# New order tables for the four engines of a decode kernel with two attention and two MLP layers

## The chip, the cores and the metric

The kernel runs on one core of a Trainium2 chip. Its time is the device time in microseconds (us), as the median of several executions. A core has five engines that run side by side, each through its own list of instructions in order: PE (TensorE, matrix products), DVE (VectorE), ACT (ScalarE), POOL (GpSimd) and SP (SyncE, which here issues the loads). They wait for each other with semaphores. Sixteen DMA engines move data between the chip's memory (DRAM) and the core's own memory (SBUF); PE writes its results into eight banks of PSUM.

## What is computed

Eight sequences with one new token each (x is 8 x 448) go through attention, MLP, and the same attention and the same MLP again, each with a layer norm ahead of it and its input added:

```
def _A_ref(x, k_cache, v_cache, wq, wo):       # Hq 16, Hkv 8, Dh 256
    W = min(4096, max(256, Sk // 4))           # the last 1024 of 4096 keys
    q = (x @ wq).reshape(B, Sq, Hq, Dh)
    scores = einsum("bhqd,bhkd->bhqk", q, k) * (Dh ** -0.5)
    p = softmax(scores)
    return einsum("bhqk,bhkd->bhqd", p, v).reshape(B, Sq, Hq * Dh) @ wo
def _B_ref(x, w1, w2):
    return silu(x @ w1) @ w2
x = x + _A_ref(layernorm(x), K, V, wq, wo);  x = x + _B_ref(layernorm(x), w1, w2)
x = x + _A_ref(layernorm(x), K, V, wq, wo);  x = x + _B_ref(layernorm(x), w1, w2)
```

Both attention layers read the same K and V. These are 8 sequences x 8 heads x 1024 keys x 256 numbers in bfloat16, for K and for V: 128 pieces of 512 KB. With the weights, 77.7 MB are read.

## The kernel before

**Tiling.** A batch b is one of the eight sequences. Its 16 pieces (8 of K, then 8 of V, one a key head) are loaded once, each into one of 33 slots of SBUF; both layers use them while they are there. Piece number n goes to slot n mod 33, so a load waits until the piece 33 places earlier, from two batches before, has been read for the last time. `pump` hands out the slots; SP issues the loads in the order of the sequence: x, wq, K of batch 0, wo, V of batch 0, w1, w2, then K and V of batches 1 to 7.

**Stages of a batch**, with the names that the text uses (`name@b` is the task of batch b):

- `KHk` (L591): each K piece is transposed in its slot by DVE, in two halves, as 32x32 blocks; 16 half transposes a batch.
- `S0.0`, `S0.1` (L611): scores of the first layer for heads 0 to 3 and 4 to 7, four tasks of 8 matmuls each. They use the query `qbd`, which for the first layer POOL spreads out (`qbd1`, L580).
- softmax: `max0`, `mT0`, `mg0`, `mb0` on DVE (L625 to L629), `exp0` on ACT (L632), `perm0` on PE (L634), `turn0` on DVE (L638), `l0` on PE (L640) and `rl0`, the reciprocals, on DVE (L643).
- values: `PV0` (two tasks, L667) and `PV4` to `PV7` (L678) on PE; `oev0`, `oevt` on ACT (L648), `oT0`, `oTt` on PE (L649), `oTev0`, `oTevt` on DVE (L652) bring the result into columns. In the last batch `PVc` and `oTc7` (L689, L694) take the last head.
- `wo` (four tasks, L736), `rowb1` (ACT, L1074), `fold1` (PE, L475), and in the last batch `woc` (L752).
- the MLP, `chain`: `xb1` (DVE, L766), `stat1`, `w1` (PE, L774, L486), `var1`, `tanh` (ACT), `pow1` (POOL, L781), `yT`, `hT` (DVE, L501, L790), `w2` (two tasks, PE, L807), `rowb2` (ACT, L811), `fold2` (PE), `xb2` (DVE), `x2b` (ACT).
- the second layer's query: `stat2`, `wq0`, `wq1` (PE, L832), `rmask` (ACT, L819), `qTa`, `qm0`, `qm1` (DVE, L501, L840), `qd` (PE, L843), `qbdw` (ACT, L847).
- the second layer: `S1.0`, `S1.1` (L611), its softmax (`max1` to `rl1`) and its values (`PV1.0`, `PV1.1`, two tasks each, L702), `oev1`, `oT1`, `oTev1`.

The second layer's wo and MLP are done for batches 0 to 5 together (`wo8`, `rowb8`, `xinit8`, `fold8`, `x8b`, `xc8`, `sq8`, `sqh8`, `stat8`, `w18`, `yT8`, `z8`, `h8`, `w28`, `rowb9`, `fold9`) and for 6 and 7 as a pair (`woL` and the names with an L, `xr`, `xres`). The last batch's second layer works on two groups of heads with their own softmax (`maxg1`, `maxg0` and so on). `idle` tasks are matmuls of 512 columns whose result nobody reads.

**Order.** The program adds its tasks in the order in which they are written. For each of PE, DVE, ACT and POOL a table, `ORDER` (L16), then says in which order that engine runs its own: each character is the place (0 to 9, a to z, A to Z) of the next task in the list of those still left. `Plan.schedule` reads the tables, and `Plan.emit` works out the semaphore waits that the dependencies need. The two score buffers, the PSUM banks and the slots are shared, so two tasks that use the same one depend on each other in program order; the tables can only move tasks between such constraints. A bank counts as in use by one engine at a time, so a read by ACT also waits for a read of the same bank by DVE. An engine never passes over a task that isn't ready.

## Time and profile before

| | us |
|---|---|
| median of 3 runs (lowest, highest) | 232.49 (232.43, 232.64) |
| the profiled execution | 232.87 |
| its span, first to last instruction | 231.1 |

| engine | busy us | share of the span |
|---|---|---|
| PE | 161.0 | 70% |
| DVE | 142.2 | 62% |
| ACT | 55.1 | 24% |
| POOL | 22.7 | 10% |

The busy sums say which engine works most, not what holds the kernel up. To see that, one looks at stretches of the span and at the waits. The profile's views used here: the page, with rows of 40 equal slices (5.8 us each) and the groups of instructions; the table of stretches (busy time, granted PE clock, share of the DMA engines and GB/s between two moments); the timeline, in which neighbouring instructions of one kind are merged, and the last bracket of a row is the engine's idle time before it and what ended it; the waits; and the chain of work that ended last. `L` and a number is a line of the kernel, and many tasks share the line of a helper.

### The profile page before, as it was taken

The numbers are of one execution on the slowest core, as the hardware profiler recorded it, in microseconds if no ns is written. First come the engines' busy times: TensorE is split into PE (matmuls) and PEld (weight loads), VectorE is DVE, ScalarE is ACT, GpSimd is POOL, SyncE is SP. The second block draws the span as 40 slices with busy tenths as digits, with TensorE's granted clock in tenths as the row PEclk, the third lists the DMA queues.
The fourth block names the chain that finished last, engine by engine and source line by source line (L and its number), as shares of the span: only waits on it lengthen the run. The fifth ranks groups of instructions, "written<-read, shape, count | busy, mean of one in ns | idle before, by whom it ended". The sixth has DMA issues, their size and how long they took to land.

```text
span 231.1 us, 7935 instructions
## 1 busy us (share of the span) xinstructions
PE 161.0 (70%) x3539; PEld 86.0 (37%) x3539; DVE 142.2 (62%) x398; ACT 55.1 (24%) x140; POOL 22.7 (10%) x41
## 2 busy tenths in 40 slices
PE   0261071854897868886887779769878877899883
PEld 0060030321363336333543353335435333565542
DVE  6828935012984696559639945983995796343623
ACT  2200000122012322132223212332322223325341
POOL 1110111000002003000300110120003000000201
PEclk9999999995559999889999999999999999999998
DMA  6999999999999999999899999999999999400000
GB/s 237 379 357 407 382 393 406 405 341 410 405 408 413 415 408 407 410 406 408 355 362 415 408 367 406 413 410 354 415 414 405 396 409 410 189 3 3 3 3 4
DMA packets 22829, 78.22 MB, mean 338 GB/s; under 512 B 2430, under 2 KB 5388, under 8 KB 22412
## 3 DMA queue, kind: packets, MB, share of 16 engines
q1 hardware_dynamic: 22772, 77.71, 86.2%
q8 instruction: 28, 0.46, 0.8%
q10 hardware_dynamic: 24, 0.01, 0.1%
q14 instruction: 5, 0.04, 0.0%
HBM read 77.70 MB, written 0.01 MB: 336 GB/s over the span
## 4 chain that ended last, share of the span: by engine, by line
PE 36%; DVE 29%; SPq 16%; DMA 9%; ACT 5%; issue 3%; POOL 0%; DVEq 0%; ACTq 0%
DVE slot L591 20%; SPq L443 10%; PE bank L611 10%; DMA w_sb<-in_B_w_dram 6%; SPq L403 5%; PE bank L702 4%; PE bank L667 3%; PE bank L832 3%; PE bank L736 2%; DVE bank L501 2%; PE bank L678 2%; DMA slot<-in_A_k_cache_dram 2%; ACT qbd L847 2%; PE bank L486 2%; DVE mm L625 1%
## 5 line engine op out<-in xcount | busy, mean ns | idle before, releaser
L591 DVE STREAM_TRANSPOSE slot<-slot 128x512 uint32<-128x512 uint32 x128 | 80.7, 679 | 7.9 <-DMA slot<-in_A_k_cache_dram 7.5
L611 PE MATMUL bank<-slot,qbd 128*8 128x256 bf16 (+1 forms) x1024 | 42.0, 300 | 14.1 <-DVE slot L591 10.4
L611 PEld LDWEIGHTS bank<-slot,qbd 128*8 128x8 bf16 (+1 forms) x1024 | 26.9, 98 | 24.7 <-DVE slot L591 13.8
L781 POOL TENSOR_TENSOR fcols<-fcols 128x1 f32<-128x1 f32 x16 | 8.7, 546 | 147.6 <-ACT fcols L779 147.6
L632 ACT ACTIVATE E<-bank,mm 128x256 bf16<-128x256 f32 x17 | 8.1, 474 | 46.9 <-DVE mm L629 41.1
L832 PE MATMUL bank<-wq_sb,xz 128*2 128x512 bf16 x224 | 16.1, 420 | 2.8 <-DVE xz L766 2.8
L702 PE MATMUL bank<-slot,pT 128*8 128x512 bf16 (+1 forms) x224 | 16.9, 412 | 1.5 <-DVE pT L638 1.5
L625 DVE TENSOR_REDUCE mm<-bank 128x1 f32<-128x256 f32 x17 | 7.2, 423 | 17.1 <-PE bank L611 17.0
L648 ACT ACTIVATE obuf<-bank 128x512 bf16<-128x512 f32 x16 | 9.6, 597 | 30.8 <-PE bank L667 20.7
L501 DVE STREAM_TRANSPOSE bank<-bank 128x448 f32<-128x448 f32 (+2 forms) x19 | 12.3, 649 | 5.9 <-PE bank L486 4.1
L652 DVE TENSOR_TENSOR q1s<-bank,q1s 128x16 bf16<-128x16 f32 (+2 forms) x25 | 4.0, 164 | 19.3 <-PE bank L649 19.1
L678 PE MATMUL bank<-slot,pT 128*12 128x512 bf16 (+3 forms) x124 | 12.5, 416 | 4.5 <-DMA slot<-in_A_v_cache_dram 3.2
L736 PE MATMUL bank<-wo_sb,q1s 128*1 128x448 bf16 x252 | 15.2, 352 | 0.5 <-DVE q1s L652 0.5
L638 DVE STREAM_TRANSPOSE pT<-bank 128x256 bf16<-128x256 bf16 x17 | 7.6, 445 | 11.2 <-PE bank L634 11.1
L580 POOL TENSOR_TENSOR qbd<-q1s,fcols 128x256 bf16<-128x256 bf16 x16 | 9.7, 613 | 33.9 <-PE bank L611 18.3
L807 PE MATMUL bank<-w_sb,hT 128*1 128x448 bf16 x112 | 8.1, 378 | 6.6 <-DVE hT L790 4.0
L667 PE MATMUL bank<-slot,pT 128*4 128x512 bf16 x128 | 10.1, 411 | 0.6 <-DVE pT L638 0.4
L766 DVE SCALAR_TENSOR_TENSOR xz<-bank,fcols 128x5 bf16<-128x5 f32 x16 | 3.3, 208 | 10.4 <-PE bank L477 10.0
L475 PE MATMUL bank<-selb,obuf 128*128 128x32 bf16 x85 | 5.0, 180 | 6.3 <-ACT obuf L811 3.5
L779 ACT ACTIVATE fcols<-bank,fcols 128x1 f32<-128x1 f32 x16 | 4.2, 261 | 19.6 <-PE bank L774 19.6
L486 PE MATMUL bank<-w_sb,xz 128*1 128x448 bf16 (+2 forms) x160 | 7.5, 313 | 1.5 <-DMA w_sb<-in_B_w_dram 1.0
L702 PEld LDWEIGHTS bank<-slot,pT 128*8 128x8 bf16 (+1 forms) x224 | 5.5, 95 | 7.4 <-DVE pT L638 2.1
(164 smaller groups left out, 196.2 us busy)
## 6 DMA issues: line engine op xcount, KB each, us to landing
slot<-in_A_k_cache_dram SPq DMA_DIRECT2D x64, 512.0 KB, 9.3
slot<-in_A_v_cache_dram SPq DMA_DIRECT2D x64, 512.0 KB, 12.4
wo_sb<-in_A_wo_dram SPq DMA_DIRECT2D x1, 3584.0 KB, 23.5
wq_sb<-in_A_wq_dram SPq DMA_DIRECT2D x3, 1024.0 KB, 7.1
w_sb<-in_B_w_dram SPq DMA_DIRECT2D x1, 1568.0 KB, 15.0
w_sb<-in_B_w_dram SPq DMA_DIRECT2D x1, 1344.0 KB, 18.2
wq_sb<-in_A_wq_dram SPq DMA_DIRECT2D x8, 64.0 KB, 7.6
w_sb<-in_B_w_dram SPq DMA_DIRECT2D x8, 32.0 KB, 11.3
```

Of the source, the lines that this page charges most:

```text
L403: dma(lambda e, h=h, r=r: e.dma_start(w[64 * h + r:64 * h + r + TAIL, :], src[3 * P + r:3 * P + r + TAIL, h * (src.shape[1] - m):h * (src. ...
L443: dma(lambda e: e.dma_start(slots[s][:, :].rearrange("p (u d) -> p u d", d=DH), cache[b, kvh, S0:SK, :].rearrange("(p u) d -> p u d", p=P) ...
L486: fns.append(lambda e: e.matmul(bank[bi][32 * t:32 * t + n, 64 * g0:64 * g1], lhs(c), view(w1_sb[:], off + 256 * g0 + 64 * t, [(256, g1 - ...
L501: dve(lambda e: e.transpose(bank[bi][:, 0:n], bank[bi][:, 0:n]), bk(bi), bk(bi), row, name)
L580: pool(lambda e, k2=k2: e.tensor_tensor(qdata(0, k2), q1s[:, b, 64 * k2:64 * k2 + 64].rearrange("p (n r) -> p n r", r=2).unsqueeze(3) .bro ...
L591: dve(lambda e, w=w: e.transpose(w, w), SL(s, h), SL(s, h), b, "KH%d" % k)
L611: fns.append(lambda e, w=w, j=j, kv=kv, cb=cb, par=par: e.matmul(sc[32 * j:32 * j + up_to, 0:256], w, kv, start=(cb == 0 and par == 0), st ...
L667: pe([lambda e, u=u, j=j: e.matmul(bank[OB[0]][32 * j:32 * j + 4, 0:512], keys2(0, u, j, 1), vals2(b, j, u), start=(u == 0), stop=(u == 3) ...
L678: pe([lambda e, t=t, kvh=kvh, m=m: e.matmul(bank[SC[0]][32 * t:32 * t + 4 * m, 0:512], keys2(0, t, kvh, m), vals2(b, kvh, t), start=True, ...
L702: pe([lambda e, u=u, j=j, k2=k2: e.matmul(bank[OB[1]][32 * j:32 * j + 8 - 4 * k2, 0:512], keys2(1, u, 4 * k2 + j, 2 - k2), vals2(b, 4 * k2 ...
L736: fns.append(lambda e, i=i: e.matmul(bank[XB][32 * (i % 4):32 * (i % 4) + 1, 0:D], oT(i), wo_row(i), start=(i < 4), stop=(i >= 28), tile_p ...
L832: fns.append(lambda e, c=c, j=j, x=x, off=off, k2=k2: e.matmul(bank[bi][32 * j:32 * j + 2, 0:512], xz[1][:, 3 * x + 1 - k2:3 * x + 3 - k2] ...
```

## The change

The tasks, the loads, the buffers and all code but the tables stay as they are. The four tables are new: they come from a search over orders in which every load from wo on counted as landed one microsecond later than it did in the search that gave the old tables.

```diff
 ORDER = {
     "pe": (
-        "00uu0000011111k11111726251910201000000000110l100201110000022220g1f221c4b033026200001100000055501001b"
+        "00uuu00s00c1000000000000403020100000000001000030222201100222203g100d5500993022040001001111660504100b"
...
     "dve": (
-        "jwcp9h1sr8tq5bme69c3hfpk18p76i4l1haah64fbeeaeee0ca7124476102289936309880672062012000000D000000006553"
+        "p1E6k8rasg4nzpn7w1u5kb8jg14og988d3ig2a7e9bcjc4dddb5225853333366633576026677443422222222D222226251464"
...
     "act": (
-        "1011110000000000020000000001100100000000100000000000010001000000001100000000000110010000040020110117"
-        "161511010323201010000"),
+        "1111000000000000001000000001000100000000100000000000010001000000001100000000000110000000003020110111"
+        "151001100323201110000"),
     "pool": (
-        "0001032003200220022002203020022000000"),
+        "0001020003203001022003203020302000000"),
 }
```

Read task by task, the parts that the prediction speaks of are these. `#1` and `#2` are halves of a transpose or tasks of a group in program order.

```
DVE, batch 1, after turn0@1
  before: rl0 oTev0 rl1@0 KH0@2#1 oTev1@0 KH0@2#2 oTevt KH1#2 KH2#1 KH1#1 xb1
  after:  rl0 oTev0 oTevt rl1@0 KH0@2#1 KH0@2#2 KH1#1 KH1#2 oTev1@0 KH3#2 xb1
DVE, batch 1, from hT@1
  before: hT KH4#2 KH4#1 KH5#2 KH6#2 xb2 KH5#1 KH7#2 KH7#1 KH6#1 qTa
  after:  hT KH4#2 KH5#2 KH5#1 KH6#1 KH7#2 xb2 KH6#2 KH7#1 KH4#1 qTa
DVE, batch 2, from yT@2
  before: yT KH4#2 hT KH4#1 KH5#1 KH6#1 KH7#2 xb2 KH6#2 KH7#1 KH5#2 qTa
  after:  yT hT KH5#2 KH7#1 KH7#2 xb2 KH5#1 KH6#1 KH6#2 qTa
DVE, batch 3, from xb1@3
  before: xb1 KH1#2 KH3#2 oTev1@2 KH3#1 yT hT KH4#1 KH4#2 KH5#1 KH5#2 xb2
  after:  xb1 oTev1@2 KH2#2 KH3#2 yT KH4#1 hT KH5#2 KH4#2 KH6#2 KH5#1 xb2
PE, batch 2, from S1.1@1#1
  before: S1.1@1#1 #2 #3 PV0@2#1 #2 S1.1@1#4 l0@2 oT0 PV4 perm1@1 PV5 xinit PV6 l1@1 PV1.0@1 PV7
  after:  S1.1@1#1 xinit S1.1@1#2 #3 #4 l0@2 PV0@2#1 #2 PV4 perm1@1 PV5 oT0 PV1.0@1#1 PV6 PV1.0@1#2 l1@1 PV7
PE, batch 3, from S1.1@2#4
  before: S1.1@2#4 l0@3 PV4 PV0#1 PV0#2 PV5
  after:  S1.1@2#4 PV0#1 l0@3 PV4 PV0#2 PV5
PE, batch 5, from oTt@5
  before: oTt l1@4 xinit wo#3 wo#4 PV1.0@4#1 #2 PV1.1@4#1 #2 fold1
  after:  oTt xinit PV1.0@4#1 #2 wo#3 wo#4 PV1.1@4#1 #2 fold1
DVE, batch 7, from oTev0@6
  before: KH0@7#1 oTev0@6 turn1@5 KH1#2 KH1#1 KH2#2 oTevt@6
  after:  oTev0@6 turn1@5 KH0@7#1 KH0#2 KH1#1 KH1#2 oTevt@6
ACT, end, from tanh@7
  before: tanh rowb8 rowb2 x8b x2b sq8 var2 rmask oev1@6 qbd2.1 qbd2.0 expg1
  after:  tanh rowb2 x2b rowb8 var2 oev1@6 rmask qbd2.1 x8b qbd2.0 sq8 expg1
```

## The prediction

> **What bounds the kernel now.** First the page: the span, PE's granted clock and the transfers in 40 slices, the largest group of VectorE.

> ```profile
> span 231.1 us, 7935 instructions
> ...
> PEclk9999999995559999889999999999999999999998
> DMA  6999999999999999999899999999999999400000
> ...
> L591 DVE STREAM_TRANSPOSE slot<-slot 128x512 uint32<-128x512 uint32 x128 | 80.7, 679 | 7.9 <-DMA slot<-in_A_k_cache_dram 7.5
> ```

> The 16 DMA engines are full from the start to slice 34 and then have nothing left to bring. So the time is a stream, plus what is still to be computed when its last piece lands. How even the stream is, the table of stretches tells (columns: length, PE busy, granted clock, DMA share, GB/s).

> ```profile
> 54.00:113.00 59.00, 46.97 (x908) 0.84 1.03 409
> 113.00:117.00 4.00, 2.81 (x83) 1.00 0.75 269
> 136.00:138.00 2.00, 1.11 (x40) 1.00 0.86 287
> 157.00:159.00 2.00, 1.89 (x56) 1.00 0.91 295
> 179.00:180.00 1.00, 1.00 (x22) 1.00 0.86 307
> 198.00:231.10 33.10, 27.31 (x722) 0.98 0.04 16
> ```

> At 409 GB/s the stream is full. Four times it runs dry; the lost time is (409 − rate) / 409 × length: 1.37, 0.60, 0.56 and 0.25 us, **2.78 us** in all. After 198 us come 33.1 us without a stream: the tail. Why it runs dry, SyncE's timeline and its waits say.

> ```profile
> 114.79 3.28 SPq L443 DMA_DIRECT2D slot<-in_A_k_cache_dram  x7
> ...
> 136.01 3.33 SPq L443 DMA_DIRECT2D slot<-in_A_k_cache_dram  x7
> ...
> 157.22 3.89 SPq L443 DMA_DIRECT2D slot<-in_A_k_cache_dram  x7
> ...
> 177.79 3.25 SPq L443 DMA_DIRECT2D slot<-in_A_k_cache_dram  x7
> ```
> ```profile
> SPq L443 <- PE bank L611: 59.8, 7, 13.0
> ```

> Each dry spell lies at one of these issues: the stream is full again, at 117, 138, 159 and 180 us, some 2 us after each. SyncE can't issue the K loads of batch b+2 before the second layer's scores of batch b (L611) have read the slots. I call that moment the release of b; those above are of b = 2, 3, 4, 5. So on the path lies, before each release, the chain of batch b: its last V load, values, wo, the MLP, the new query, S1.0. Everything else there is hidden by the stream.

> **The change, part by part.** Read task by task, the tables differ in many places: 245 of 435 of PE hold another task, 328 of 398 of DVE, 24 of 121 of ACT, 12 of 37 of POOL. No instruction is added or removed, no byte and no load changes, SyncE keeps its order. So the sum is about the four releases and the tail.

> The start of the chain of work comes first.

> ```profile
> 39.07 14.97 DMA w_sb<-in_B_w_dram
> ...
> 54.17 1.67 PE bank L807 x11
> ```
> ```profile
> 124.29 0.93 PE L486 MATMUL bank<-w_sb,xz 128*1 128x448 bf16 x20
> ```

> In the chain that ended last, PE's first w2 waits for the load of w2. Whatever is reordered before it (the constants, q1sel, four idle tasks moved ahead of q1, PV0@0) costs nothing so long as it is done by 54.04; I take 0. If the idle tasks' new place left PE at half speed there, w1@0 would take as long again as a w1 at full speed, the second row's 0.93 us, and could use up this cover; any more of it would put release 2 back.

> *Release of 2.* Three views bear on it: the stretches around a drop of the clock, PE's timeline, and DVE's.

> ```profile
> 93.07:96.48 3.41, 2.59 (x50) 1.00 1.03 411
> 96.48:99.90 3.42, 3.42 (x36) 0.50 1.02 402
> 185.23:188.64 3.41, 1.86 (x47) 1.00 1.03 413
> ```
> ```profile
> 94.65 0.42 PE L678 MATMUL bank<-slot,pT 128*16 128x512 bf16 x4 [0.63 <-DVE q1s L643]
> ...
> 96.35 1.82 PE L702 MATMUL bank<-slot,pT 128*8 128x512 bf16 x16
> ...
> 98.37 1.79 PE L702 MATMUL bank<-slot,pT 128*4 128x512 bf16 x16
> ...
> 122.35 1.04 PE L702 MATMUL bank<-slot,pT 128*4 128x512 bf16 x16
> ```
> ```profile
> 83.07 2.47 DVE L591 STREAM_TRANSPOSE slot<-slot 128x512 uint32<-128x512 uint32 x4
> ...
> 106.42 2.49 DVE L591 STREAM_TRANSPOSE slot<-slot 128x512 uint32<-128x512 uint32 x4 [0.23 <-issue]
> ```

> A half transpose (KH) occupies DVE for 0.62 us (2.47 / 4). Later: in batch 1 the new table puts all KH of batch 2 behind both value evictions (two of them stood among these before), and five instead of four between hT and xb2. That is one to three KH, 0.6 to 1.9 us; I take 1.5, as DVE has no gap to take them in there. Earlier: both sets of 16 PV1 matmuls of batch 1 ran at half clock, 1.82 + 1.79 − 2 × 1.04 = 1.5 us; I count on that not coming back (rival below). The 0.63 us wait of PE: S1.1@1 now stands ahead of PV0@2, so the reciprocal is sooner; −0.3, between 0 and −0.6. In batch 2 no KH stands between yT and hT, and three instead of four between hT and xb2: at most −1.2, and since tanh and fold2 also end there, −0.7. Sum 1.5 − 1.5 − 0.3 − 0.7 = **−1.0 us**; bounds −2.2 and +1.0.

> [...]

> *Release of 3.* A wait of PE, and one of DVE's own operations that comes late:

> ```profile
> 116.68 0.41 PE L678 MATMUL bank<-slot,pT 128*16 128x512 bf16 x4 [0.71 <-DVE mg L627]
> ```
> ```profile
> 125.90 0.62 DVE L501 STREAM_TRANSPOSE bank<-bank 128x448 f32<-128x448 f32 x1
> ```

> PE idles 0.71 us; the new table puts half of PV0@3 there: 8 matmuls of 512 columns, half of the 1.04 above or a little less, −0.4. yT@3 starts 0.68 us after w1 ended (124.29 + 0.93), behind three KH; now two stand there: −0.6, of which one KH put between yT and hT gives back 0.2. S1.0@2 is no longer cut by perm0@3: −0.1. stat2 now stands ahead of wq0 and waits for x2b: +0.2. Own sum −0.7, on top of the −1.0: **−1.7**. Bounds of its own part: −1.2 and 0.

> *Release of 4.* turn0 moves ahead of max1 on DVE, PV0's halves and PV4 to PV7 change places, and five KH stand between the last eviction and xb1@4. By count the gain and the loss are each one KH or so; I take 0, bounds ±0.6: still **−1.7**.

> *Release of 5.* PE's timeline, then ACT's:

> ```profile
> 163.57 1.90 PE L702 MATMUL bank<-slot,pT 128*8 128x512 bf16 x32
> ...
> 165.41 0.29 PE L475 MATMUL bank<-selb,obuf 128*128 128x32 bf16 x5
> ```
> ```profile
> 163.80 0.54 ACT L1074 ACTIVATE obuf<-bank 128x448 bf16<-128x448 f32 x1 [1.56 <-PE bank L736]
> 164.24 0.20 ACT L1074 ACTIVATION_READ_ACCUMULATOR obuf<-bank 128x1 bf16 x1
> ```

> rowb1@5 is done at 164.44, but fold1 waits 1.0 us behind 32 PV1 matmuls. Half of these now stand ahead of the last two wo groups: −0.9 behind wo, up to +0.9 before it, less the wait for the eviction that they fill. I take −0.6, bounds −0.9 and 0: **−2.3**.

> *What the stream gets back.* A dry spell closes by what its release gains over what the stream has gained by then. First: 1.0 of 1.37. Second: 1.7 − 1.0 = 0.7, enough for 0.60; the stream is 1.6 ahead. Third: 1.7 − 1.6 = 0.1; 1.7. Fourth: 2.3 − 1.7 = 0.6, enough for 0.25. **1.95 us**.

> *Tail.* ACT's timeline, then DVE's:

> ```profile
> 207.79 0.54 ACT L904 ACTIVATE slot<-bank 128x448 bf16<-128x448 f32 x1
> 208.22 0.20 ACT L904 ACTIVATION_READ_ACCUMULATOR slot<-bank 128x1 bf16 x1
> ...
> 212.27 0.30 ACT L819 ACTIVATE fcols<-fcols 128x4 f32<-128x4 f32 x1 [0.66 <-POOL fcols L781]
> 212.47 0.58 ACT L648 ACTIVATE qbd<-bank 128x512 bf16<-128x512 f32 x1
> ```
> ```profile
> 211.19 0.18 DVE L506 CAST slot<-slot 128x24 bf16<-128x24 f32 x1
> ...
> 212.63 0.16 DVE L507 TENSOR_TENSOR slot<-slot 128x24 bf16<-128x24 f32 x1
> ```

> rowb8 ran in a gap of ACT; now it stands between x2b@7 and var2@7 and, with oev1@6, ahead of rmask: its 0.74 us puts var2 back by 0.3, of which rmask's slack before qm1 leaves 0.1. sqh8's two operations (0.34 us) move in among the maxima of S1@7, where the exponent waits for them: 0.15. Fewer S1@6 matmuls stand ahead of the last wo, but oTc7 now waits behind max1@6, and woc for it: 0. **+0.25 us**; bounds −0.2 and +0.6. The swaps of xr, rowb9, fold9, h8 and of POOL's qbd1 with pow2 lie beside waits for tanh, for ACT and for the scores; I cost them at nothing, and at one such operation each if that cover goes.

> *Sum*: −1.95 + 0.25 = −1.7. The profiled execution took 232.87 us (span 231.1), 0.38 above the median of 232.49; the gain is carried over to the median: **230.8 us**.

> **The rivals.** *The half clock comes back* in the chain of 2 or 3: then release 2 is 0.5 late instead of 1.0 early and the first spell grows by 0.5; release 3, at −0.2, still closes its 0.60 (stream +0.1 ahead), 4 and 5 add 0.35. Gain 0.45 − 0.25: 232.3. For it: what sets it off isn't seen in the busy time. Against: after slice 12 the clock row of the page shows one such dip.

> *Slower: DVE in batch 7.* The first half transpose of that batch:

> ```profile
> 181.54 0.71 DVE L591 STREAM_TRANSPOSE slot<-slot 128x512 uint32<-128x512 uint32 x1 [1.28 <-DMA slot<-in_A_k_cache_dram]
> ```

> This KH0@7 filled a wait for exp1@5; now it follows turn1@5, and 16 instead of 15 KH lie between that and S0.1@7: +0.6, and the tail's 0.25: 233.3. It decides if the releases gain nothing, so that the K of batch 7 lands when it did; if the loads land 0.6 us sooner, it is paid for.

> *All spells close* and the tail costs nothing: 232.49 − 2.78 = 229.7. For it: the releases need only 2.8 us in all. Against: the third finds no gain in my count.

> **How the numbers follow.** Forecast (230.2 to 231.8) 0.50; half clock (to 232.7) 0.20; slower 0.15; all spells 0.15. The range leaves out the slower case and the edge below: 229.8 to 232.8. A measurement can tell 0.2%, 0.46 us, from no change: faster than 232.03 are the forecast, the all-spells case and a little of the half-clock one, 0.68; within 0.2% the rest of that, 0.17; slower 0.15.

> **What would show it.** In the changed profile the stretches at 113 and 136 us have a DMA share of 1.0, SyncE issues the K loads of these releases 1 to 2.3 us sooner, and the transfers fall off some 2 us before 198 us; from there to the end takes 0.2 us more. Wrong if the share drops stay, if a 0.50 clock appears after 72 us, or if the loads end sooner and the end doesn't move: then the tail bounds, not the stream.

## The result, and the profile after

231.19 us, median of 20 runs (230.41 to 232.64), against 232.46 of 20 runs before (231.37 to 235.36) on the same chip: ratio 0.995, 95% interval 0.9926 to 0.9974. That is 1.3 us less, where the prediction had 1.7. The profiled execution after the change took 232.64 us, the longest of the 20, and its trace has to be read with that in mind. Its page, the lines that answer to those shown of before:

```profile
span 230.6 us, 7931 instructions
...
PEclk9999999995559999999999999999999997999998
DMA  6999999999999999999999999999999999200000
...
L591 DVE STREAM_TRANSPOSE slot<-slot 128x512 uint32<-128x512 uint32 x128 | 81.3, 681 | 10.3 <-DMA slot<-in_A_k_cache_dram 10.3
```

In slice 34 the transfers are down to two tenths instead of four, and the clock row, which had its dip in slices 16 and 17, has it in slice 33 (counted from 0). The table of stretches of the same trace (length, PE busy, weight loads, DVE, ACT, POOL, granted clock, DMA share, GB/s):

```profile
93.00:96.00 3.00, 2.70 (x61) 1.33 (x60) 1.09 (x6) 0.90 (x2) 0.00 (x0) 1.00 1.01 374
113.00:117.00 4.00, 3.31 (x82) 1.88 (x72) 1.78 (x7) 0.99 (x2) 0.00 (x0) 1.00 1.01 397
136.00:138.00 2.00, 1.83 (x32) 0.75 (x32) 0.94 (x5) 0.47 (x1) 0.00 (x0) 1.00 1.03 410
157.00:159.00 2.00, 1.94 (x44) 0.90 (x40) 0.46 (x4) 1.27 (x3) 0.00 (x0) 1.00 1.01 401
179.00:180.00 1.00, 1.00 (x24) 0.61 (x28) 0.27 (x2) 0.24 (x1) 0.00 (x0) 1.00 1.05 422
188.13:191.54 3.41, 1.70 (x38) 0.70 (x35) 2.91 (x6) 1.00 (x3) 0.39 (x1) 1.00 1.03 405
191.54:194.95 3.41, 3.41 (x67) 1.69 (x70) 1.26 (x5) 0.17 (x1) 0.00 (x0) 0.50 1.02 410
```

The four dry spells of before are gone (269, 287, 295 and 307 GB/s then); a small new one lies at 93 us, (409 − 374) / 409 × 3 = 0.26 us. In exchange the half clock is back, at 191.54 us, in batch 7. SyncE's timeline shows the releases:

```profile
113.28 3.31 SPq L443 DMA_DIRECT2D slot<-in_A_k_cache_dram  x7
...
134.05 3.38 SPq L443 DMA_DIRECT2D slot<-in_A_k_cache_dram  x7
...
155.19 3.27 SPq L443 DMA_DIRECT2D slot<-in_A_k_cache_dram  x7
...
175.42 3.48 SPq L443 DMA_DIRECT2D slot<-in_A_k_cache_dram  x7
```

They come 1.51, 1.96, 2.03 and 2.37 us sooner than before; 1.0, 1.7, 1.7 and 2.3 were predicted. The last V piece lands at 199.35 us instead of 200.96 (landings are read from the DMA events of the trace): 1.6 us gained. The span gained 0.4. So 1.2 us was lost between the last landing and the end, 31.3 us instead of 30.1. Two questions for the experiments: where was it lost, and is it the tables that moved the releases, or the half clock that left batch 1?

### The profile page after: what moved, and what is told of

It is laid out like the page before. It is cut to its first block, busy times and chain, and to the rows that moved or that the text cites. A ratio compares the mean times of both kernels' runs of the same rounds, so it can differ in the third digit from the quotient of the medians.

```text
span 230.6 us, 7931 instructions
## 1 busy us (share of the span) xinstructions
PE 159.4 (69%) x3535; PEld 86.3 (37%) x3539; DVE 142.6 (62%) x398; ACT 54.4 (24%) x140; POOL 22.7 (10%) x41
## 4 chain that ended last, share of the span: by engine, by line
PE 34%; DVE 27%; SPq 16%; DMA 12%; ACT 5%; issue 4%; POOL 0%; DVEq 0%; ACTq 0%
DVE slot L591 17%; SPq L443 10%; PE bank L611 8%; PE bank L832 7%; DMA w_sb<-in_B_w_dram 7%; DMA slot<-in_A_k_cache_dram 6%; SPq L403 4%; DVE bank L501 3%; PE bank L702 3%; PE bank L667 2%; PE bank L678 2%; PE bank L807 1%; ACT qbd L847 1%; DVE pT L638 1%; PE bank L634 1%
## 5 line engine op out<-in xcount | busy, mean ns | idle before, releaser
L591 DVE STREAM_TRANSPOSE slot<-slot 128x512 uint32<-128x512 uint32 x128 | 81.3, 681 | 10.3 <-DMA slot<-in_A_k_cache_dram 10.3
L611 PE MATMUL bank<-slot,qbd 128*8 128x256 bf16 (+1 forms) x1024 | 42.1, 303 | 13.6 <-DVE slot L591 9.8
L611 PEld LDWEIGHTS bank<-slot,qbd 128*8 128x8 bf16 (+1 forms) x1024 | 28.0, 99 | 22.3 <-DVE slot L591 11.9
L781 POOL TENSOR_TENSOR fcols<-fcols 128x1 f32<-128x1 f32 x16 | 8.7, 545 | 143.1 <-ACT fcols L779 143.1
L832 PE MATMUL bank<-wq_sb,xz 128*2 128x512 bf16 x224 | 17.0, 438 | 2.0 <-DVE xz L766 2.0
L501 DVE STREAM_TRANSPOSE bank<-bank 128x448 f32<-128x448 f32 (+2 forms) x19 | 12.5, 659 | 8.6 <-PE bank L486 3.0
L638 DVE STREAM_TRANSPOSE pT<-bank 128x256 bf16<-128x256 bf16 x17 | 7.6, 447 | 15.1 <-PE bank L634 14.9
L736 PE MATMUL bank<-wo_sb,q1s 128*1 128x448 bf16 x252 | 15.8, 359 | 1.4 <-DVE q1s L652 1.4
L648 ACT ACTIVATE obuf<-bank 128x512 bf16<-128x512 f32 x16 | 9.5, 596 | 29.6 <-PE bank L667 21.4
L702 PE MATMUL bank<-slot,pT 128*8 128x512 bf16 (+1 forms) x224 | 15.6, 380 | 0.7 <-DVE pT L638 0.6
L580 POOL TENSOR_TENSOR qbd<-q1s,fcols 128x256 bf16<-128x256 bf16 x16 | 9.7, 612 | 36.7 <-PE bank L611 27.8
L678 PE MATMUL bank<-slot,pT 128*12 128x512 bf16 (+3 forms) x124 | 11.8, 406 | 1.2 <-DVE mm L626 0.5
L807 PE MATMUL bank<-w_sb,hT 128*1 128x448 bf16 x112 | 8.1, 378 | 6.3 <-DVE hT L790 3.6
L475 PE MATMUL bank<-selb,obuf 128*128 128x32 bf16 x85 | 5.0, 180 | 6.1 <-ACT obuf L811 3.4
L486 PE MATMUL bank<-w_sb,xz 128*1 128x448 bf16 (+2 forms) x160 | 7.5, 313 | 1.9 <-DMA w_sb<-in_B_w_dram 1.4
L811 ACT ACTIVATE obuf<-bank,fcols 128x448 bf16<-128x448 f32 x8 | 5.1, 634 | 12.5 <-PE bank L807 5.9
L1074 ACT ACTIVATE obuf<-bank 128x448 bf16<-128x448 f32 x8 | 4.3, 542 | 15.1 <-PE bank L736 15.1
```

The costliest lines, as they stand in the source:

```text
L501: dve(lambda e: e.transpose(bank[bi][:, 0:n], bank[bi][:, 0:n]), bk(bi), bk(bi), row, name)
L580: pool(lambda e, k2=k2: e.tensor_tensor(qdata(0, k2), q1s[:, b, 64 * k2:64 * k2 + 64].rearrange("p (n r) -> p n r", r=2).unsqueeze(3) .bro ...
L591: dve(lambda e, w=w: e.transpose(w, w), SL(s, h), SL(s, h), b, "KH%d" % k)
L611: fns.append(lambda e, w=w, j=j, kv=kv, cb=cb, par=par: e.matmul(sc[32 * j:32 * j + up_to, 0:256], w, kv, start=(cb == 0 and par == 0), st ...
L638: dve(lambda e: e.transpose(pT_sb[i], bank[tb][:, t0:t0 + 256].bitcast(BF16)[:, 1:512:2]), bk(tb), pT, b, "turn" + nm)
L678: pe([lambda e, t=t, kvh=kvh, m=m: e.matmul(bank[SC[0]][32 * t:32 * t + 4 * m, 0:512], keys2(0, t, kvh, m), vals2(b, kvh, t), start=True, ...
```

## The experiments

Twelve runs were made. Two repeat the kernels without an edit; seven are mixtures, most with the new tables up to a cut and the old ones from there, or the reverse; three add work to the changed kernel. At each cut the same tasks have been done in both orders but for a few next to it, so a mixture changes no task either. One table collects their traces. All times are in us from the last V landing of batch 0, since that lands between 44.2 and 45.8 us from one execution to the next, whatever the kernel. "Half clock" lists the stretches at 0.50 after 70 us (absolute times, without the last ones at the very end); "release 2" is the end of S1.0@2; "K to max" the time from the last K landing of batch 7 to its first maximum, max0@7.

| kernel | half clock | release 2 | last V | K to max | end | time, ratio to before (95%) |
|---|---|---|---|---|---|---|
| before | 96.5–99.9 | 69.96 | 156.18 | 4.09 | 186.31 | |
| before_again | 188.4–195.2 | 68.34 | 155.35 | 5.68 | 186.86 | one run |
| the change | 191.5–195.0 | 68.45 | 154.56 | 4.01 | 185.86 | 0.995 (0.9926–0.9974) |
| after_again | until 70.3 | 69.06 | 155.28 | 3.45 | 184.61 | 0.992 (0.989–0.995) |
| newstream_oldtail | 83.7–87.1 | 68.60 | 154.67 | 3.46 | 184.40 | 0.994 (0.992–0.997) |
| oldstream_newtail | 71.7–75.1 | 69.44 | 155.97 | 4.13 | 185.65 | 0.997 (0.994–1.001) |
| new_to_release2 | none | 67.78 | 154.68 | 4.04 | 185.16 | 0.998 (0.995–1.001) |
| old_to_release2 | 96.1, 150.7, 184.8 | 69.91 | 157.25 | 4.99 | 187.72 | 0.9945 (0.991–0.998) |
| old_to_release5 | none | 68.01 | 154.18 | 4.41 | 185.03 | 0.997 (0.994–1.000) |
| after_w1_twice | none | 68.42 | 154.89 | 3.54 | 184.54 | 0.991 (0.988–0.995) |
| dve_only_to_release2 | none | 69.50 | 155.53 | 4.08 | 186.05 | 1.000 (0.998–1.003) |
| others_only_to_release2 | none | 69.17 | 155.37 | 4.16 | 185.27 | 1.004 (1.002–1.007) |
| after_idle6 | none | 68.18 | 154.39 | 3.39 | 184.13 | 0.996 (0.994–0.998) |
| after_w1_four | none | 70.29 | 156.17 | 3.43 | 185.98 | 1.0015 (0.998–1.005) |

(The trace of old_to_release2 is of an execution with a span of 232.2 us; the median span of its runs was 229.7.)

**The tail.** First the changed kernel once more, without an edit.

> The changed kernel once more, for a second trace of it. The stream theory (the releases close the dry spells, and the tail is as long as before) expects the last landing at 199.0 to 199.7 us again, no half clock between 185 and 200 us this time or at another place, and with it some 30.2 us from the last landing to the end, so a span near 229.5 and a time near 231.2 us. The tail theory (the new order of batch 7 and the tail itself loses the 1.1 us between landing and end that the first trace shows) expects again 31 us or more from the last landing to the end, whatever the clock does there. The clock theory (the gain is where the half clock happened to fall, not the releases) expects the K loads after 113 us to be issued at other moments than in the first trace, by 1 us or more.

231.35 us. The last landing came at 201.07, not by 199.7: batch 0 had landed 1.0 later, and the half clock of the start lasted until 70.3 us instead of 68.7, which put the end of S1.1@0 another 0.6 later; the span, 230.4, is also above the expected 229.5. The same two amounts make the loads at 113.28 us come 1.6 later here, at 114.90. But with no half clock in batch 7 only 29.3 us lie between last landing and end, as against 31.3 us. The tail theory falls: the 1.2 us were the clock's. PE's timeline, first of the change, then of after_again:

```profile
192.96 1.92 PE L832 MATMUL bank<-wq_sb,xz 128*2 128x512 bf16 x16
```
```profile
193.64 1.09 PE L832 MATMUL bank<-wq_sb,xz 128*2 128x512 bf16 x16
```

This is wq0@6, with wq1@6 behind it and then perm0@7 of the last batch: 0.83 us lost on this one task.

Then the two halves, cut at the maximum of batch 7. newstream_oldtail, against the change:

```diff
...
     "act": (
-        "1111000000000000001000000001000100000000100000000000010001000000001100000000000110000000003020110111"
-        "151001100323201110000"),
+        "1111000000000000001000000001000100000000100000000000010001000000001100000000000110000000040020110117"
+        "161511010323201010000"
```

> The new order on all engines up to the scores of the first layer of batch 7 (from there, the old one). Stream theory: K loads issued and last landing as in the changed kernel (199.0 to 199.7 us), time 0.0 to 0.3 us below it (the prediction's +0.25 for the tail is taken back), so 230.9 to 231.3 against 232.5 before. Tail theory: 0.8 us or more below the changed kernel, 230.4 or less.

oldstream_newtail, against before, is the reverse:

```diff
...
     "act": (
-        "1011110000000000020000000001100100000000100000000000010001000000001100000000000110010000040020110117"
-        "161511010323201010000"),
+        "1011110000000000020000000001100100000000100000000000010001000000001100000000000110010000003020110111"
+        "151001100323201110000"
```

> The old order on all engines up to the scores of the first layer of batch 7, from there the new one. Stream theory: dry spells as before the change, last landing 200.8 to 201.1 us, time 0.0 to +0.4 us against before. Tail theory: +0.8 us or more. If the new tail is itself better, below before by 0.3 us or more.

231.36 us for the first, as much as the changed kernel, 232.77 for the second against 232.95 of before on that chip: what the tables change in the tail is worth nothing that can be measured. The traces say it more sharply: from xb1@7 to the end it is 25.64 us before, 25.63 with the old tail and 25.65 with the new one, 25.78 and 25.75 in the two traces of the change. Of the predicted +0.25 at most 0.14 is there.

**Release 2.** The first release by itself, and everything but it. new_to_release2 against before, and old_to_release2 the reverse:

```diff
     "pe": (
-        "00uu0000011111k11111726251910201000000000110l100201110000022220g1f221c4b033026200001100000055501001b"
-        "bbb00007000055023504130772660100010107770050100bbbb000800000028336204131620002011002188811001001bgbb"
+        "00uuu00s00c1000000000000403020100000000001000030222201100222203g100d5500993022040001001111660504100b"
+        "bbb00080006000222504193802662000000007770050100bbbb000006000028336204131620002011002188811001001bgbb"
...
```

> The new order on all engines until the second layer's scores of batch 2 have read their K slots, the old order from there. Stream theory: the first dry spell (113 to 117 us, 1.37 us) is gone, those at 136, 157 and 179 us stay, only sooner; K loads issued some 1.4 us sooner at each release, last landing 199.6 to 200.1 us, time 0.9 to 1.4 us below before (231.1 to 231.6). The prediction's own numbers: release 2 alone gains 1.0, so 231.5. If the first release is not what counts (tail or clock theory): within 0.3 us of before.

> The old order on all engines until the second layer's scores of batch 2 have read their K slots, the new one from there: the counterpart of the run that had the new order up to this point. Stream theory: the dry spell at 113 to 117 us stays, releases 3 to 5 gain about 0.45, 0.1 and 0.4 us on the one before, which closes the spells of 0.60 and 0.25 in part: last V landing of batch 7 0.4 to 0.8 us sooner than before, measured from the last V landing of batch 0 (156.2), max0@7 0.6 us sooner still, time 0.8 to 1.3 us below before. If the first release is worth nothing, as much as the whole change: 1.3 us or more.

The trace of the first did as expected, last V at 154.68 instead of 156.18. Its time did not: 232.26 us, 0.998, nothing that can be told from before. The second gave 231.45, 0.9945, as much as the whole change. Both are on the side of "the first release is worth nothing", against my theory, though the interval of the first leaves room for half a per cent. The table shows another thing: the latest releases 2 of unmixed tables, 69.44 to 69.96, all belong to traces with a half clock shortly before (70.29 is that of a kernel with added work, below).

**Clock or order.** So the kernel before was profiled again, unchanged.

> The kernel before, once more, for a second trace with the half clock perhaps at another place. All times from the last V landing of batch 0. Clock theory of the stream (the order before reaches release 2 early enough at full clock, and the dry spells come from a half clock in batch 0, 1 or 2): if no 0.50 lies between 70 us and release 2, release 2 at 67.7 to 68.3 us (69.96 in the first trace) and the last V landing at 154.2 to 154.9 (156.18); if one lies there, 69.4 to 70.0 and 155.9 to 156.3. Order theory (the old order itself makes release 2 late): 69.4 or later and 155.9 or later in both cases. In both, max0@7 4.0 to 4.2 us after the last K landing of batch 7.

Release 2 came at 68.34, 1.6 us sooner, by the same tables. PE's timelines of the two traces of before agree to 0.1 us up to the moment when the clock falls in one of them; here is before_again, to be laid beside the 1.82 and 1.79 us of the prediction's rows:

```profile
95.74 0.40 PE L678 MATMUL bank<-slot,pT 128*8 128x512 bf16 x4
96.07 0.37 PE L640 MATMUL bank<-pT,cols 128*128 128x32 bf16 x8
96.37 1.05 PE L702 MATMUL bank<-slot,pT 128*8 128x512 bf16 x16
97.24 0.39 PE L678 MATMUL bank<-slot,pT 128*4 128x512 bf16 x4
97.46 1.04 PE L702 MATMUL bank<-slot,pT 128*4 128x512 bf16 x16
```
```profile
113.00:117.00 4.00, 3.31 (x78) 1.87 (x70) 1.18 (x6) 0.99 (x2) 0.00 (x0) 1.00 1.00 387
```

With that the first dry spell is nearly closed, 387 instead of 269 GB/s, and no table was touched: SyncE issues the loads at 113.14 us instead of 114.79. The last V landing, 155.35, is later than the 154.9 expected: 0.8 us won, the rest of the 1.6 stays with the later releases. The half clock has gone to batch 7 here too and costs there more than in the change (5.68 us from K to maximum).

The other traces say the same when release 2 is counted from the end of S1.1@0, which takes out most of what the half clock before 70 us does to it. With full clock from there on it takes 44.2 and 44.7 us with wholly old tables (before_again, old_to_release5) and 44.4 to 44.7 with wholly new ones (the change, after_again, new_to_release2, after_idle6). With a half clock in between it takes 45.8 to 45.9 with old ones (before, oldstream_newtail, old_to_release2) and 45.6 with new ones (newstream_oldtail). So what moves release 2 is the clock, by 0.9 to 1.7 us; the tables move it by no more than traces of one order differ.

Which engine's table makes a difference up to release 2? DVE's alone, and the other three alone:

```diff
     "dve": (
-        "jwcp9h1sr8tq5bme69c3hfpk18p76i4l1haah64fbeeaeee0ca7124476102289936309880672062012000000D000000006553"
+        "p1E6k8rasg4nzpn7w1u5kb8jg14og988d3ig2a7e9bcjc4dddb5225853333366633576026677443422222222D222226251464"
...
```

> The kernel before with only DVE's new order, and only until the maximum of batch 3's first layer; PE, ACT and POOL keep the old order throughout. The prediction's terms for DVE: +1.5 us in batch 1 (all half transposes behind the evictions), -0.7 in batch 2 (fewer of them before hT and xb2). By these terms release 2 comes 0.8 us later than before when the half clock lies in the same place, the first dry spell grows, and the time is 0.5 to 0.8 us above before. Rival: what batch 1 loses is taken up by the wait for the last V pieces of batch 2, and only the -0.7 to -1.0 of batch 2 is left: from w1@2 to the end of S1.0@2 10.2 to 10.4 us instead of 11.2, release 2 sooner by 0.5 us or more, time 0.3 to 0.9 us below before.

> The kernel before with the new order of PE, ACT and POOL until release 2, DVE in the old order throughout: the complement of the run that had only DVE's new order (which measured no gain). If release 2 is won by the PE table: time 0.4 to 0.8 us below before and release 2 as with all four tables. If DVE and PE are worth something only together: within 0.3 us of before. If the gain at release 2 is the clock's alone: release 2 at 67.6 to 68.3 us after the last V landing of batch 0 when no 0.50 lies in batches 1 and 2, later by 0.8 us or more when one does.

DVE's alone changes nothing (1.000; neither number came), the others alone lose 0.4%, 1.0 us, which none of the expectation's cases had. In both traces release 2 is late, 69.50 and 69.17, without any half clock after 70 us; with all four new tables, and none either, it is at 67.78, and with all four old ones at 68.01 (old_to_release5). The tables only work together, and together they gain nothing here. The words "the clock's alone" of the expectation aren't met either: a mixed order makes release 2 late at full clock.

**Is the release on the path at all?** Work was added in front of it: w1 of batch 2 computed twice, and four times.

```diff
         self.order = {}
+        for t in self.tasks:
+            if (t.name, t.row) == ("w1", 2):
+                t.fns = t.fns * 2
```

> The changed kernel with the 20 w1 matmuls of batch 2 computed twice (the same values written again), 0.9 us of PE more in the chain that leads to release 2. Stream theory: this release is on the path and has almost nothing to spare after the change (396 instead of 409 GB/s at 113 to 117 us), so the later releases move with it: K loads after it 0.9 us later, last V landing 0.6 to 0.9 later, time 0.5 to 0.9 us above the changed kernel. If the stream doesn't wait for this release any more, or the clock made the gain: 0.0 to 0.2 us.

> The changed kernel with the 20 w1 matmuls of batch 2 computed four times (the same values written again), 2.8 us of PE more ahead of release 2; computed twice they cost nothing. Stream theory with slack: release 2 has to come by about 68.5 us after the last V landing of batch 0, and each microsecond later makes the last V landing later by about one. Then release 2 comes at 70.0 to 71.0 (67.8 to 69.1 without the added matmuls), a dry spell of 1.3 to 2.3 us opens after it, the last V landing is at 155.9 to 156.9, and the time 1.2 to 2.3 us above the changed kernel. If the releases are not what makes the stream dry: no dry spell, and within 0.4 us of the changed kernel.

Twice, 0.8 us more from w1 to the transposed row: release 2 at 68.42, 230.85 us, no loss. I had read 397 GB/s as "almost nothing to spare", and that was wrong. Four times, 2.3 us more: 70.29, and the dry spell opens as expected, in the table of stretches (409 GB/s is the full stream):

```profile
113.00:117.00 4.00, 3.27 (x92) 2.41 (x88) 1.78 (x8) 1.03 (x2) 0.32 (x1) 1.00 0.78 293
```

with the last V at 156.17, 1.6 later than in the change. The time, 233.04 us, is that of another chip; by the ratios to before, 1.0015 and 0.995, it is 1.5 us above the change. So the mechanism holds, with a threshold between 68.4 and 70.3: in the table, releases up to 69.2 go with a last V of 154.2 to 155.4, those of 69.4 to 70.3 with 155.5 to 157.3.

**Batch 7.** What no step of the forecast had is the column "K to max": 4.04 to 4.16 with the old order of batches 6 and 7, 3.39 to 3.54 with the new one from batch 2 or earlier on, at full clock. DVE's timeline of before and then of after_again: first turn1@5 (L638) and the half transposes beside it, then from yT@6 on. The first K piece of batch 7 lands at 181.52 and 181.47 us, the last at 190.45 and 190.41:

```profile
182.24 0.43 DVE L638 STREAM_TRANSPOSE pT<-bank 128x256 bf16<-128x256 bf16 x1
182.83 1.98 DVE L591 STREAM_TRANSPOSE slot<-slot 128x512 uint32<-128x512 uint32 x3 [0.16 <-DMA slot<-in_A_k_cache_dram]
...
190.50 0.62 DVE L501 STREAM_TRANSPOSE bank<-bank 128x448 f32<-128x448 f32 x1
191.03 0.67 DVE L591 STREAM_TRANSPOSE slot<-slot 128x512 uint32<-128x512 uint32 x1
191.63 0.13 DVE L790 SCALAR_TENSOR_TENSOR hT<-th,bank 128x14 bf16<-128x14 f32 x1
191.68 1.29 DVE L591 STREAM_TRANSPOSE slot<-slot 128x512 uint32<-128x512 uint32 x2
...
194.53 0.42 DVE L625 TENSOR_REDUCE mm<-bank 128x1 f32<-128x256 f32 x1 [0.35 <-PE bank L611]
```
```profile
181.33 0.45 DVE L638 STREAM_TRANSPOSE pT<-bank 128x256 bf16<-128x256 bf16 x1 [0.51 <-PE bank L634]
181.71 2.45 DVE L591 STREAM_TRANSPOSE slot<-slot 128x512 uint32<-128x512 uint32 x4
...
189.26 0.62 DVE L501 STREAM_TRANSPOSE bank<-bank 128x448 f32<-128x448 f32 x1
189.79 0.67 DVE L591 STREAM_TRANSPOSE slot<-slot 128x512 uint32<-128x512 uint32 x1
190.38 0.13 DVE L790 SCALAR_TENSOR_TENSOR hT<-th,bank 128x14 bf16<-128x14 f32 x1
190.43 1.88 DVE L591 STREAM_TRANSPOSE slot<-slot 128x512 uint32<-128x512 uint32 x3
...
193.86 0.42 DVE L625 TENSOR_REDUCE mm<-bank 128x1 f32<-128x256 f32 x1 [0.54 <-PE bank L611]
```

When the last K piece has landed, yT and three half transposes are still to come with the old order; with the new one three half transposes only, the first of them begun 0.02 us after the landing. DVE is done 2.52 and 1.90 us after it. What differs lies further ahead: from the landing of the first K piece to its last half transpose DVE works almost without a pause (0.19 us of idle time and none), for 11.45 us with the old order and 10.84 with the new one. The new order has oTev0@6 done and turn1@5 begun when that piece lands, in time that DVE otherwise spends waiting for it (the 1.28 us in the prediction's row). The kernel's end hangs on this: in 11 of the 14 traces it comes 36.4 to 36.6 us after max0@7 starts, and 36.7, 36.8 and 37.4 in the other three, while from the last V landing it is 29.3 to 31.5. This is the place of the rival that ended on the slower side, with the opposite sign. Its condition was tested by keeping the old order, and so the old releases, until release 5:

> The old order on all engines until the second layer's scores of batch 5 have read their K slots (release 5), from there the new one. It puts the prediction's rival on DVE in batch 7 to the test under its own condition, releases that gain nothing. Dry spells as before in every theory (last V landing 155.9 to 156.3 us after the last V landing of batch 0). Rival: KH0@7 behind turn1@5 and 16 half transposes instead of 15 cost 0.6, so the maximum of batch 7 (max0@7) starts 4.6 us after the last K landing of batch 7 (before: 4.09) and the time is 0.5 us or more above before. Arrival theory (what counts is how many half transposes are left when the last K piece of batch 7 lands, and oTev0@6 and turn1@5 placed ahead of KH0@7 are done while DVE would wait for K anyway): 3.4 to 3.6 us, and the time 0.4 to 0.8 us below before.

```diff
...
     "dve": (
...
-        "9a90006666600400c20cbc1ab90gf810ced0c0ba0999990106666000030222660534311ccc6b6155704033022021110000"),
+        "9a9000666666000020aaaa1990981ed0cc0b0aba09999900066605000302220331111ee10c05a504464002220121111000"
...
     "act": (
-        "1011110000000000020000000001100100000000100000000000010001000000001100000000000110010000040020110117"
-        "161511010323201010000"),
+        "1011110000000000020000000001100100000000100000000000010001000000001100000000000110000000003020110111"
+        "151001100323201110000"
```

K to max was 4.41 us, 0.3 above before. DVE's timeline of this kernel shows why (its lines are numbered four further on: L642 is turn1, L595 the half transposes):

```profile
180.27 0.45 DVE L642 STREAM_TRANSPOSE pT<-bank 128x256 bf16<-128x256 bf16 x1 [0.51 <-PE bank L638]
180.64 2.45 DVE L595 STREAM_TRANSPOSE slot<-slot 128x512 uint32<-128x512 uint32 x4
```

The first K piece of batch 7 had landed at 179.50, and its transposes stand behind turn1@5 until 180.64: 1.14 us late. In the change and its second trace they begin 0.0 and 0.2 us after their landing, because PE is done with perm1@5, for which turn1@5 waits, 0.4 and 0.2 us before the K piece lands; here it is done 0.7 us after it. So the rival's mechanism is real and its condition is the right one; the full change doesn't meet it. The time of this mixture speaks against it all the same, 232.09 us, 0.997, where the rival wanted 0.5 us above before and the arrival theory 0.4 to 0.8 below; why it is faster with a longer K to max stays open. In its trace, which has no half clock after 70 us, the last K piece of batch 7 lands 1.6 us sooner than in that of before (144.07 and 145.67 in the clock of the table), but one trace says little of a median.

**The half clock of batch 7.** Last, eight more idle matmuls in PE's waits of batch 6:

```diff
-IDLE = {0: (4,), 1: (3,), 2: (0,), 3: (1,), 4: (0,), 5: (0,), 6: (0,), 7: (0, 0)}
+IDLE = {0: (4,), 1: (3,), 2: (0,), 3: (1,), 4: (0,), 5: (0,), 6: (8,), 7: (0, 0)}
```

> The changed kernel with eight more idle matmuls of 512 columns in batch 6, two, four and two, each group in a wait of PE's that the trace shows (0.71, 1.05 and 0.66 us). In the traces so far a window of 3.41 us at full clock was followed by half clock when PE was given under some 11,000 columns in it, counted over its matmuls; the window before the drop at 191.54 us had 10,496. Clock theory: with about 2,000 columns more per window there is no 0.50 between 180 and 200 us, max0@7 starts 3.4 to 3.6 us after the last K landing of batch 7, and the tail never loses the 1.2 us of the first trace: a median 0.1 to 0.4 us below the changed kernel. If the count of columns is not what matters, or the added matmuls delay w2 of batch 6: the same or above, and a 0.50 can still be there.

The page of this kernel, then its stretches around the place:

```profile
span 228.4 us, 7944 instructions
...
PEclk9999999995679999999999999999999999999999
```
```profile
187.08:190.49 3.41, 3.06 (x49) 1.17 (x44) 3.28 (x7) 1.14 (x4) 0.54 (x1) 1.00 1.02 404
190.49:193.90 3.41, 3.41 (x91) 2.00 (x91) 1.25 (x5) 0.80 (x3) 0.55 (x1) 1.00 1.03 412
```

PE is busy 3.06 us there instead of 1.70, no drop follows, K to max is 3.39, and the span is the shortest of all traces. But of the seven traces with the new order of batch 6 and without these matmuls five have no half clock there either (not so the change and old_to_release2), so it isn't shown that they kept the clock up. Its median, 231.04 us, is 0.15 below that of the change, from another chip, and by the ratios to before (0.996 and 0.995) there is no gain; whether the idle matmuls are a gain stays open, and no kernel here is shown to beat the change.

## Why the prediction was right, and where not

The forecast of 230.8 us was 0.4 too low, and the sign was right. But more than half of the gain was to come from release 2, which the tables don't move, so that the number came near is in part luck. One of the prediction's own signs of being wrong showed in the profile after the change, a 0.50 clock after 72 us, and another in part: the loads end 1.6 us sooner, and the span shrinks by only 0.4. The steps at equal clock come from the pair before_again and the change: both have no half clock between 69 and 188 us, and in both batch 0 lands at 44.77 or 44.78.

- **What bounds**: right. In after_w1_four a release that comes 1.84 us later than in the change makes the last V land 1.61 later. Missing was the threshold: in after_w1_twice 0.8 us more work cost nothing.
- **The start**: 0 predicted. w2@0 started at 53.93 us instead of 54.17, S1.1@0 ended at 68.88 in both. Right.
- **Release 2**, −1.0 predicted, −1.51 in the first pair of traces. The half clock's term was right in size: −1.5 predicted, 69.96 to 68.34 = −1.62 between two traces of one kernel. But that is no work of the tables. Theirs, from before_again to the change: batch 1 +0.57 (1.5 predicted), from S1.1@1 to w1@2 +0.63 (−0.3 predicted, the wrong sign), from w1@2 to S1.0@2 −1.03 (−0.7 predicted), the start −0.06; in all +0.1. The bounds given, −2.2 and +1.0, are not those of the terms either: with 0.6 and 1.9 for batch 1, their ends add up to −2.7 and +0.4. The step that failed is "I count on that not coming back": it put into a step of the change what a second profile of the kernel before would have taken out.
- **Release 3**: its own −0.7 predicted, −0.34 measured. yT@3 came 0.6 sooner, as said; filling PE's wait gave nothing from S1.1@2 to the end of wo@3 (−0.03) and not 0.4, S1.0 uncut 0.1 as said. But xb1@3 waits longer on DVE, +0.46 from fold1 to w1, which no step had. stat2 in front of wq0 cost 0.4 instead of 0.2, and no step had that it also brings rmask sooner: from wq0 to S1.0@3 0.47 us came back.
- **Release 4**: 0 predicted, −0.06 measured. **Release 5**: −0.6 predicted, −0.47 measured. Both right.
- **What the stream gets back**: 1.95 predicted, 1.62 between the two first traces, and 0.79 between the two at equal clock.
- **Tail**: +0.25 predicted, 0 to 0.14 measured from xb1@7 on, and −0.6 from the last K landing to max0@7 at full clock. The mistake is in the frame: I let the tail begin at the last V landing. In the change PVc@7, which reads the last V piece, starts 2.1 us after that landing; what sets the end there is the K of batch 7 and what DVE has to do for it. At full clock the two lie close: in before and in after_again PVc@7 starts 0.4 and 0.2 us after the landing, so DVE could have gained little more before the last V set the end.
- **The rivals**: the half clock did come back in the profiled execution, not in batch 2 or 3 but in batch 7, where the prediction had no price for it: 185.86 − 184.61 = 1.25 us against the second trace of the change. "Slower" is told above. "All spells close" came true in the stretches named (but for 0.2 us), yet not in the time.

Put together, at equal clock the order itself is worth some 0.6 us: between before_again and the change the last K piece lands no sooner (144.45 and 144.43 in the clock of the table), so the last V's 0.79 meets the slack before PVc@7, and what is left is the K to max of batch 7. The median gained 1.3. Where the rest comes from stays open. One candidate is the place of the half clock: between 71 us and release 2 one shows in three of the six traces that have the old PE table up to there, and in one of the eight that have the new one. But the counts are small, and the medians lean the other way: old_to_release2, with the old tables up to there, gained as much as the whole change, and new_to_release2, with the new ones, gained nothing that can be told from before. Nor did the runs after the change get more clock: on the chip of after_again the mean granted clock was 0.953 in its 12 runs and 0.951 in 35 of before, and of the runs at 0.96 or more the spans were 229.3 us in the mean (6 runs) and 230.5 (9). The mixtures can't divide the rest either: their intervals are some 0.3% to either side, and the whole gain is 0.5%.

## What to carry to other kernels

Before a gain is put down to an order of instructions, take a second profile of the kernel before and lay the two clock rows side by side: here the same tables moved a release by 1.6 us between two executions. The deadline of the releases had a threshold here, between 68.4 and 70.3 us, and 0.8 us more work on its early side (after_w1_twice) cost nothing: so ask of each step whether it lies on the late side. At the end of a stream look at the piece that has the most work behind it, not at the piece that lands last, count what is left in its engine's queue when it lands, and put other work of that engine into its wait for the first of these pieces.

## What the runs showed of the hardware

The last V piece of batch 0 landed 44.2 to 45.8 us after the start of the span, in 14 traces that load the same bytes in the same order. Such a difference, of up to 1.5 us, is as large as the effect in question; only times taken from that landing on could be compared between traces.
